# Keys of pair 5 transposed at the end of pair 4, between two stretches of feed-forward units

## Chip, cores and metric

The kernel runs on one core of one Trainium2 chip. The metric is the device time of one execution in microseconds (us), as a median over runs.

## What is computed

Attention over 4 batches of 8 heads, 768 positions and 64 values each, then a feed-forward block over the 3072 tokens that result:

```
scores = q @ k.T / sqrt(64)
mask   = causal                                  for heads 0, 2, 6   ("retrieval" heads)
         causal and (key < 4 or distance < 64)   for the other five  ("streaming" heads)
attn   = softmax(scores, masked) @ v             (4 x 8 x 768 x 64)
x      = attn, heads side by side                (3072 x 512)
h      = x @ w_in                                (3072 x 2048)
g      = max(h, 0) + alpha * min(h, 0)           (alpha: one number per column)
out    = g @ w_out                               (3072 x 512)
```

Inputs and output are float32; the kernel multiplies in bf16.

## The kernel before

Attention goes by pairs of heads: 16 pairs, n = 0 to 15, four in each batch, in the order (0,1), (2,3), (6,7), (4,5). Pair 4 is heads 0 and 1 of the second batch, pair 5 is heads 2 and 3. Each has a retrieval head first and a streaming head second. The work of a pair, by function:

- `load(n)` issues the loads of queries, keys and values (tiles `qf`, `kf`, `vf`) on SP's DMA queue. Up to pair 7, keys of each head are a DMA of their own.
- `whole_q(n)`, `whole_k(n)`, `whole_v(n)` cast them to bf16 (`natq`, `natm`, `vb`). POOL does it for pairs 1 to 5. For pairs 6 and 7 ScalarE (ACT) casts the queries (L162), VectorE (DVE) the keys (L175) and values (L189).
- `Tq(n)` and `Tk(n)`, for pairs up to 7, transpose queries and keys on TensorE (PE): six 128x128 transposes each (L265) into a PSUM bank. ScalarE copies the queries to `qT` (L275). Of the keys, ScalarE copies those of the first head to `kT` (L288) and, after it, VectorE those of the second (L292 to L294). From pair 8 on, DMAs transpose instead.
- `Sr(n,h,i)` and `Ss(n,h,i)`, short here for calls of `S_retr` and `S_stream`, compute one piece of the scores: matmuls with `kT` and `qT` (L333, L360) into one of two PSUM banks that alternate, an exponential on ScalarE (L341, L367), and a mask product on VectorE (L345, L371). From pair 4 on a retrieval head has six pieces, a streaming head three.
- `AV(n,h)` multiplies with the values (L387), then a reciprocal and a product on VectorE (L392, L393). `X(n)` transposes the pair's result (L400) into `xT` (L402).

The feed-forward part goes by token tiles t = 0 to 7, of 512 and 256 tokens in turn, in units. `P1(t,f)` is a block of the first matrix (L431), with a relu on ScalarE (L438) and one or two operations on VectorE (L441). `P2(t,s,u)` is a quarter of a 128-token row block of the second (L451); after the last quarter ScalarE copies the block (L456) and it is stored.

Every engine works through its instructions in the order in which the program issues them. For pairs 4 to 15 a planner sets that order. It has a list of *pieces* (the calls above, from `seg_pieces(n)`), with casts and loads ahead of pieces 0, 2 and 4 of a pair, and a list of *units*. It goes through the pieces. After each it adds to a budget the units left divided by the pieces left up to the next change of plan, and issues units while the budget holds half a unit's cost (L624 to L639). So a piece more, even an empty one, shifts all units up to the end of that plan a little. The first plan has 26 units and reaches into pair 8.

For pair 4 the order of pieces is written out by itself, since no pair before it overlaps:

```
sa + sb[:1] + [AV(4,0)] + [Tq(5), Tk(5)] + sb[1:]
```

with `sa` the six pieces of head 0 and `sb` the three of head 1. With the units that the planner puts between them, the program has from there on

```
AV(4,0)  P2(0,0,1)  Tq(5)  Tk(5)  P1(1,2)  Ss(4,1,1)  Ss(4,1,2)  P2(0,1,1)
whole_q(6)  Sr(5,0,0)  AV(4,1)  P2(0,0,2)  whole_k(6)  Sr(5,0,1)  Sr(5,0,2)  P1(1,4) ...
```

Of the kernel before, what the change touches and what calls it, by code (L numbers as in the profile page):

```python
# [14 lines left out]
def kernel(  # L15
# [51 lines left out]
    def bank(tag):  # L67
        return P[:, BANK[tag], :]
# [36 lines left out]
    def heads(n):  # L105
        return PAIRS[n % 4]
# [151 lines left out]
    def misc_tag():  # L258
        n_misc[0] += 1
        return f"m{n_misc[0] % 2}"  # L260
# [11 lines left out]
    def Tq(n):  # L272
        tr = T_bank(natq.pop(n), "mm0" if n < 4 else misc_tag())
        T = row_tokens(n)
        nc.scalar.copy(qT[n % NK][:, 0:S].rearrange("d (p t) -> d p t", t=T), in_order(tr[:, 0:S], T))  # L275

    def Tk(n):
        tr = T_bank(natk.pop(n), "mm1" if n < 4 else misc_tag())
        for hh, h in enumerate(heads(n)):
            T = row_tokens(n, h)  # L280
            rows = slice(64 * hh, 64 * hh + 64)
            kt = kTs[n % NK][hh][rows, :]
            src = in_order(tr[rows, 0:S], T)
            copy = nc.scalar.copy if n >= 4 and hh == 0 else nc.vector.tensor_copy
            if RETR[h]:
                cuts = [0, -(-256 // T), S // T] if n == 0 else [0, S // T]
                for lo, hi in zip(cuts, cuts[1:]):
                    copy(kt[:, 0:S].rearrange("d (p t) -> d p t", t=T)[:, lo:hi, :], src[:, lo:hi, :])  # L288
                continue
            slots = kt.rearrange("d (j m t) -> d j m t", j=7, t=T)  # L290
            a, z = NSINK // T, 748 // T
            copy(slots[:, 0:6, a:128 // T, :], src[:, a:z, :].rearrange("d (j m) t -> d j m t", j=6))  # L292
            nc.vector.tensor_copy(slots[:, 6, a:24 // T, :], src[:, z:S // T, :])
            nc.vector.tensor_copy(slots[:, :, 0:a, :], src[:, 0:a, :].unsqueeze(1).to_broadcast([64, 7, a, T]))  # L294
# [80 lines left out]
    def AV(n, hh):  # L375
        e, vv = ebuf.pop((n, hh)), vb[n % NV]
        pav = bank(misc_tag())[:, 0:NT * (D + 1)].rearrange("p (i c) -> p i c", c=D + 1)
        for i in range(NT):
            if RETR[heads(n)[hh]]:
                terms = [(RO[j] + QS[i] - QS[j], j) for j in range(min(i, 5) + 1)]  # L380
            elif i == 0:
                terms = [(0, 0)]
            else:
                own = SLOT * i + 4 if i < 6 else 5 * SLOT + 152
                terms = [(SLOT * (i - 1) + 128, i - 1), (own, i)]
            for m, (o, j) in enumerate(terms):
                nc.tensor.matmul(pav[:, i, :], e[:, o:o + 128], vv[:, j, hh, 0:D + 1],  # L387
                                 start=(m == 0), stop=(m == len(terms) - 1))
        if hh == 0:
            xn[n] = work.tile([128, NT, 128], bf16, tag="xn", name="xn")  # L390
        rcp = work.tile([128, NT, 1], fp32, tag=f"rcp{hh}", name="rcp")
        nc.vector.reciprocal(rcp, pav[:, :, D:D + 1])  # L392
        nc.vector.tensor_tensor(xn[n][:, :, 64 * hh:64 * hh + 64], pav[:, :, 0:D],  # L393
                                rcp.to_broadcast([128, NT, D]), op=ALU.mult)

    def X(n):
        nat = xn.pop(n)
        tr = bank_bf(misc_tag())
        for i in range(NT):
            nc.tensor.transpose(tr[:, QS[i]:QS[i] + 128], nat[:, i, :], ident)  # L400
        o = n // 4 % 2 * S
        nc.vector.tensor_copy(xT[:, n % 4, o:o + S], tr[:, 0:S])  # L402
# [79 lines left out]
    def seg_scores(n):  # L482
        parts = []
        for hh, h in enumerate(heads(n)):
            fn, m = (S_retr, N_R) if RETR[h] else (S_stream, 3)
            if n < 4:
                m = -(-m // 2)
            parts.append([lambda m=m, hh=hh, fn=fn: fn(n, hh, m) for m in range(m)])
        return parts

    def seg_pieces(n):
        sa, sb = seg_scores(n)

        prev = [lambda: AV(n - 1, 1)] if n > 4 else []
        tail = [lambda: X(n - 1)] if n > 4 else []
        nxt = [lambda: Tq(n + 1), lambda: Tk(n + 1)] if n + 1 < CROSS else []
        seq = sa[:1] + prev + sa[1:3] + tail + sa[3:5] + nxt[:1] + sa[5:] + nxt[1:] + sb[:1]
        seq += [lambda: AV(n, 0)] + sb[1:]
        if n == 4:
            seq = sa + sb[:1] + [lambda: AV(n, 0)] + nxt + sb[1:]  # L500
        return seq, (2 + len(sa[1:3]) if tail else 0)

    whole_q(0)
# [42 lines left out]
    for n in range(4):  # L546
        sa, sb = seg_scores(n)
        last = [lambda: AV(n - 1, 0), lambda: AV(n - 1, 1), lambda: X(n - 1)] if n else [None] * 3
        nxt = [lambda: Tq(n + 1), lambda: Tk(n + 1)] if n < 3 else [None] * 2
        if len(sa) == 3:  # L550
            seq = [sa[0], last[0], nxt[0], sa[1], last[1], nxt[1], sa[2], sb[0], last[2], sb[1]]
        else:
            seq = [sa[0], last[0], sa[1], last[1]] + sb + [lambda: AV(3, 0), last[2]]
        if n == 0:
            seq = sa[:2] + nxt[:1] + sa[2:] + nxt[1:] + sb
        if n == 0:
            seq += [slopes, factors]
        seq = [x for x in seq if x]
# [32 lines left out]
    for n in range(4, NSEG):  # L591
        seq, x_at = seg_pieces(n)
        for i, piece in enumerate(seq):
            pre = []
            if i in (0, 2, 4):
                fn = (whole_q, whole_k, whole_v)[i // 2]
                pre = [lambda m=m, fn=fn: fn(m) for m, lo, hi in ((n + 1, 5, CROSS), (n + 2, CROSS, NSEG)) if lo <= m < hi]
            if i == 4 and n < NSEG - NF:
                pre.append(lambda n=n: load(n + NF))
            ready = []  # L600
            if x_at and i == x_at - 1 and n % 4 == 0:
                ready = [n // 2 - 2, n // 2 - 1]
            pieces.append((pre, piece, ready))
# [75 lines left out]
```

## Time and profile before

| | us |
|---|---|
| median of 5 runs | 246.24 |
| the five | 245.63 to 246.52 |
| the profiled execution | 247.28 |
| its span, first to last instruction | 245.3 |
| PE busy in it | 232.7 (95%) |
| DVE, ACT, POOL busy | 165.5, 142.9, 48.7 |

The profile comes from one execution, which took 1.04 us more than the median of the others. Times in it count from the start of its span. A busy share of PE counts matmuls that overlap as one stretch. In the lists of groups and in the timeline a row gives the engine, the line of the kernel, the operation, what it writes and reads, and how many; in brackets stands the idle time of the engine before it and what released it. "PEld" is TensorE's weight load and "PEclk" the share of its clock that was granted. The page also cuts the span into 40 slices of 6.13 us, one digit each, in tenths.

### The profile page before, as it was taken

How to read it: one execution, taken by the hardware profiler on the slowest of the kernel's cores; microseconds unless marked ns; L12 is line 12 of the kernel's file. 1: busy time of each engine (PE TensorE's matmuls, PEld its weight loads, DVE VectorE, ACT ScalarE, POOL GpSimd, SP SyncE). 2: the span in 40 equal slices, each digit the busy share in tenths (PEclk: the TensorE clock that was granted, in tenths of full speed). 3: DMA queues.
4: the chain of work that ended last, by engine and by line, in shares of the span. 5: the costliest groups of instructions: out<-in, count | busy, mean ns of one | idle time of the engine just before them, and what ended most of it. 6: DMA issues, size and time to landing. Idle time of an engine off the chain costs nothing.

```text
span 245.3 us, 5348 instructions
## 1 busy us (share of the span) xinstructions
PE 232.7 (95%) x2059; PEld 146.6 (60%) x2059; DVE 165.5 (67%) x398; ACT 142.9 (58%) x255; POOL 48.7 (20%) x98
## 2 busy tenths in 40 slices
PE   7799899949999999999999999999999999999994
PEld 6688545636677645556766555556676544465553
DVE  7788788836789968888577767876665556542310
ACT  5888188656876658665554467765655255533320
POOL 5669610720230310201111100300000000000000
PEclk9999999988999999999999999999999999999999
DMA  7999999999999999999969930501111101012112
GB/s 223 283 238 171 226 201 204 243 262 250 244 217 140 246 155 229 222 181 230 182 143 175 229 83 9 141 3 43 45 43 47 43 0 43 3 43 85 46 44 86
DMA packets 85377, 34.95 MB, mean 142 GB/s; under 512 B 72536, under 2 KB 83560, under 8 KB 85352
## 3 DMA queue, kind: packets, MB, share of 16 engines
q1 hardware_dynamic: 79368, 25.36, 51.9%
q0 software_dynamic: 5664, 8.91, 16.3%
q10 hardware_dynamic: 320, 0.34, 0.5%
q8 instruction: 16, 0.26, 0.4%
q14 instruction: 9, 0.07, 0.1%
HBM read 27.46 MB, written 6.29 MB: 138 GB/s over the span
## 4 chain that ended last, share of the span: by engine, by line
PE 67%; DMA 12%; DVE 8%; SPq 5%; ACT 3%; issue 2%; POOL 2%; DVEq 0%; ACTq 0%; POOLq 0%
PE P L451 27%; PE P L431 26%; DMA kf<-in_k_dram 7%; PE P L387 5%; PE P L333 3%; DMA qf<-in_q_dram 3%; PE P L360 3%; DMA vf<-in_v_dram 2%; SPq L141 2%; SPq L139 2%; DVE g L441 2%; PE P L468 1%; DVE vb L189 1%; SPq L126 1%; ACT eR L341 1%
## 5 line engine op out<-in xcount | busy, mean ns | idle before, releaser
L441 DVE SCALAR_TENSOR_TENSOR g<-neg,oma,P 128x512 bf16<-128x512 f32 (+1 forms) x128 | 74.9, 612 | 49.7 <-ACT neg L438 48.2
L431 PE MATMUL P<-xT,w_in_b 128*128 128x512 bf16 (+1 forms) x512 | 96.2, 326 | 1.2 <-DVE xT L402 1.2
L451 PE MATMUL P<-w_out_b,g 128*128 128x512 bf16 x368 | 93.5, 382 | 0.0
L438 ACT ACTIVATE neg<-P 128x512 f32<-128x512 f32 x96 | 57.1, 597 | 54.3 <-PE P L431 50.7
L431 PEld LDWEIGHTS <-w_in_b 128*128 128x128 bf16 x512 | 48.2, 98 | 28.9
L451 PEld LDWEIGHTS <-g 128*128 128x128 bf16 x368 | 33.8, 98 | 29.0 <-issue 1.2
L341 ACT ACTIVATE eR<-P 128x455 bf16<-128x455 f32 (+3 forms) x63 | 37.4, 604 | 13.8 <-PE P L333 11.9
L367 ACT ACTIVATE eS<-P 128x384 bf16<-128x384 f32 (+1 forms) x55 | 27.7, 520 | 10.5 <-PE P L360 9.9
L459 POOL DMA_DIRECT2D out_dram<-ot x18 | 10.3, 574 | 100.8 <-ACT ot L456 93.5
L333 PE MATMUL P<-qT,kT 128*128 128x454 bf16 (+10 forms) x132 | 24.4, 271 | 1.1 <-DVE kT L288 0.5
L371 DVE TENSOR_TENSOR eS<-eS,ms 128x384 bf16<-128x384 bf16 (+1 forms) x47 | 17.8, 389 | 4.4 <-ACT eS L367 4.1
L360 PE MATMUL P<-qT,kT 128*128 128x192 bf16 (+2 forms) x140 | 20.0, 237 | 0.8 <-ACT eR L341 0.6
L393 DVE TENSOR_TENSOR xn<-P,rcp 128x448 bf16<-128x448 f32 x32 | 20.0, 625 | 1.1
L456 ACT COPY ot<-P 128x512 f32<-128x512 f32 x23 | 13.5, 585 | 10.4 <-PE P L451 10.4
L333 PEld LDWEIGHTS <-kT 128*128 128x128 bf16 x132 | 11.6, 98 | 11.6 <-issue 2.4
L360 PEld LDWEIGHTS <-kT 128*128 128x128 bf16 x140 | 13.2, 99 | 8.3 <-issue 0.3
L345 DVE TENSOR_TENSOR eR<-eR,mr 128x128 bf16<-128x128 bf16 (+4 forms) x54 | 11.6, 235 | 4.7 <-ACT eR L341 4.6
L387 PEld LDWEIGHTS <-eS 128*128 128x128 bf16 x260 | 11.0, 99 | 4.1 <-issue 0.8
L387 PE MATMUL P<-vb,eS 128*128 128x65 bf16 x260 | 12.3, 196 | 0.6 <-DVE eS L371 0.4
L387 PEld LDWEIGHTS <-eR 128*128 128x128 bf16 x324 | 11.3, 97 | 1.3
L387 PE MATMUL P<-vb,eR 128*128 128x65 bf16 x324 | 11.9, 192 | 0.0
L292 DVE COPY kT<-P 64x744 bf16<-64x744 bf16 x9 | 8.4, 933 | 4.2 <-ACT kT L288 4.0
(81 smaller groups left out, 157.8 us busy)
## 6 DMA issues: line engine op xcount, KB each, us to landing
qf<-in_q_dram SPq DMA_DIRECT2D x16, 384.0 KB
vf<-in_v_dram SPq DMA_DIRECT2D x32, 192.0 KB
kf<-in_k_dram SPq DMA_DIRECT2D x31, 192.0 KB
out_dram<-ot POOLq DMA_DIRECT2D x18, 256.0 KB, 3.1
w_in_b<-in_moe_w_in_dram POOLq DMA_DIRECT2D x4, 512.0 KB, 8.6
w_out_b<-in_moe_w_out_dram POOLq DMA_DIRECT2D x4, 512.0 KB, 19.4
out_dram<-ot SPq DMA_DIRECT2D x5, 256.0 KB
vf<-in_v_dram SPq DMA_DIRECT2D x20, 6.0 KB
```

The source lines that it names most:

```text
L333: nc.tensor.matmul(sc[:, x, a - lo:z - lo], kt[:, 128 * j:128 * (j + 1)], qt[:, c:c + z - a], start=True, stop=not masked)
L341: nc.scalar.activation(e[:, lo:hi].rearrange("p (x c) -> p x c", x=len(parts)), sc[:, 0:len(parts), 0:(hi - lo) // len(parts)], AF.Exp, sc ...
L360: nc.tensor.matmul(sc[:, x, o:o + w], kt[:, 128 * j:128 * (j + 1)], qt[:, 124 * j:124 * j + w], start=True, stop=not on_pe)
L367: nc.scalar.activation(slots, sc[:, 0:len(thirds), 0:384].rearrange("p x (s c) -> p x s c", c=192), AF.Exp, scale=scale)
L371: nc.vector.tensor_tensor(slots, slots, factor, op=ALU.mult)
L387: nc.tensor.matmul(pav[:, i, :], e[:, o:o + 128], vv[:, j, hh, 0:D + 1], start=(m == 0), stop=(m == len(terms) - 1))
L393: nc.vector.tensor_tensor(xn[n][:, :, 64 * hh:64 * hh + 64], pav[:, :, 0:D], rcp.to_broadcast([128, NT, D]), op=ALU.mult)
L431: nc.tensor.matmul(psg[:, w * i:w * (i + 1)], w_in_b[:, a, 128 * fb:128 * (fb + 1)], xT[:, c, o:o + w], start=(c == 0), stop=(c == 3))
L438: nc.scalar.activation(neg, psg, AF.Relu, scale=-1.0)
L441: nc.vector.scalar_tensor_tensor(g_buf[t % 2][:, fb, 0:w], neg[:, c], oma[:, fb:fb + 1], psg[:, c], op0=ALU.mult, op1=ALU.add)
L451: nc.tensor.matmul(bank(po[t, s]), g_buf[t % 2][:, f, 128 * s:128 * (s + 1)], w_out_b[:, f, :], start=(f == 0), stop=(f == 15))
L456: nc.scalar.copy(ot, bank(po.pop((t, s))))
```

## The change

The order of pieces for pair 4. `Tq(5)` stays behind `AV(4,0)`. `Tk(5)` goes behind the two remaining pieces of pair 4's second head, with an empty piece ahead of it and one behind it. Empty pieces issue nothing, but the planner may put units after them.

```diff
         if n == 4:
-            seq = sa + sb[:1] + [lambda: AV(n, 0)] + nxt + sb[1:]
+
+            seq = sa + sb[:1] + [lambda: AV(n, 0)] + nxt[:1] + sb[1:] + [lambda: None] + nxt[1:] + [lambda: None]
         return seq, (2 + len(sa[1:3]) if tail else 0)
```

By the planner's arithmetic the order of the program becomes

```
AV(4,0)  P2(0,0,1)  Tq(5)  Ss(4,1,1)  P1(1,2)  Ss(4,1,2)  P2(0,1,1)  Tk(5)  P2(0,0,2)
whole_q(6)  Sr(5,0,0)  AV(4,1)  P1(1,4)  whole_k(6)  Sr(5,0,1)  P2(0,1,2)  Sr(5,0,2)
whole_v(6)  load(9)  X(4)  Sr(5,0,3)  Sr(5,0,4)  P2(0,0,3)  Tq(6)  Sr(5,0,5)  P1(1,6)  Tk(6)  Ss(5,1,0) ...
```

and further units change places with the piece beside them up to `Tk(7)`. Which unit uses which PSUM bank stays as it was.

## The prediction

> **What bounds the kernel now.** I read the page first, then TensorE's waits, then the time around the change on TensorE, POOL and ScalarE, then stretches of one clock window each. The page's busy shares and slices:
>
> ```profile
> PE 232.7 (95%) x2059; PEld 146.6 (60%) x2059; DVE 165.5 (67%) x398; ACT 142.9 (58%) x255; POOL 48.7 (20%) x98
> ...
> PE   7799899949999999999999999999999999999994
> ...
> PEclk9999999988999999999999999999999999999999
> ```
>
> TensorE (PE) is busy almost everywhere, so the sum of its work and its gaps is the time. One slice after the start-up shows 4 tenths (the ninth, 49.1 to 55.2 us), and the only clock digits of 8 stand there and in the next slice. The waits of PE name the cause:
>
> ```profile
> PE P L265 <- POOL natm L175: 3.2, 1, 3.2
> ...
> PE P L387 <- DVE eS L371: 0.4, 1, 0.4
> ```
>
> One wait of 3.2 us: the transposes of `Tk(5)` for the cast of pair 5's keys. All other waits of PE after start-up are at most 0.6 us each. PE in order of time (start, length, idle before):
>
> ```profile
> 48.48 0.50 PE L265 MATMUL P<-ident,natq 128*128 128x128 bf16 x6
> 52.14 0.51 PE L265 MATMUL P<-ident,natm 128*128 128x128 bf16 x6 [3.16 <-POOL natm L175]
> 52.49 1.04 PE L431 MATMUL P<-xT,w_in_b 128*128 128x256 bf16 x8
> 53.36 0.74 PE L360 MATMUL P<-qT,kT 128*128 128x192 bf16 x5
> 53.92 1.88 PE L451 MATMUL P<-w_out_b,g 128*128 128x512 bf16 x4
> 55.60 0.59 PE L333 MATMUL P<-qT,kT 128*128 128x454 bf16 x1
> ```
>
> `Tq(5)` is followed by nothing until the keys come. Directly behind `Tk(5)` in PE's queue stands work that doesn't read them: `P1(1,2)` (L431), the last two score pieces of pair 4 (L360), `P2(0,1,1)` (L451). The keys' side, on POOL and on ScalarE:
>
> ```profile
> 51.58 0.51 POOL L175 CAST natm<-kf 128x384 bf16<-128x384 f32 x1 [2.77 <-DMA kf<-in_k_dram]
> ...
> 52.69 0.79 ACT L288 COPY kT<-P 64x768 bf16<-64x768 bf16 x1 [2.87 <-PE P L265]
> ...
> 54.85 0.84 ACT L162 CAST natq<-qf 128x768 bf16<-128x768 f32 x1
> ```
>
> The second head's keys land at 51.53 and POOL casts them at once. That time belongs to the DMA and not to PE, so PE being earlier or later doesn't move it. Stretches of 3.41 us (length; busy us of PE, PEld, DVE, ACT, POOL; clock; DMA share, GB/s) show the price behind the gap:
>
> ```profile
> 46.65:50.06 3.41, 2.32 (x39) 1.52 (x36) 3.06 (x7) 1.46 (x3) 2.16 (x4) 1.00 1.20 231
> 50.06:53.47 3.41, 1.33 (x16) 1.24 (x17) 0.00 (x0) 0.78 (x1) 0.51 (x1) 1.00 1.08 309
> 53.47:56.88 3.41, 3.41 (x25) 2.03 (x23) 2.62 (x8) 2.63 (x6) 1.27 (x2) 0.50 0.74 193
> ```
>
> After the stretch with PE busy for 1.33 of 3.41 us (39%) the clock is halved for a whole stretch, while PE has work throughout: 3.41 x 0.5 = 1.7 us lost. After the stretch with 2.32 us (68%) it is not. That is why the L451 group above takes 1.88 us instead of the usual 1.02.
>
> **What the Trainium skill says.** "TensorE: Matmul & The Clock Gate", Part 1, says that the clock is set by a free-running window of 3413 ns and falls to one half after an idle window. The trace agrees on length and half rate; it differs on "idle", since 39% of busy time was not enough here, and the measurement decides. The same page's specification table calls ScalarE and VectorE strict FIFOs, on which I rely where a cast that waits for a transfer holds up an exponential behind it. The trace lists both engines' instructions in program order at this place, which agrees but doesn't prove it.
>
> **The change part by part.** It removes and adds no instruction: the two empty pieces emit nothing. The planner's spacing of units shifts, which I worked out by following its arithmetic: bank names stay the same, and the order differs only from `Tk(5)` to about `Tk(7)`.
>
> 1. *The gap.* By start times the gap is from 48.48 + 0.34 = 48.82 to 52.14, 3.32 us. Now `Ss(4,1,1)`, `P1(1,2)`, `Ss(4,1,2)`, `P2(0,1,1)` stand in it. At full clock, from rows of the same shapes elsewhere: 0.17 + 0.87 + 0.17 + 0.86 = 2.07 us, to 50.89. Their inputs are ready: the values of g(0) long since, score banks free at 47.3. `Tk(5)` still starts at 52.14, so 1.25 us of gap stays. **Gain 2.07 us.**
>
> 2. *The clock.* The stretch from 50.06 to 53.47 then holds 1.33 + 0.83 = 2.2 us of PE, 63%, close to the 68% that kept the clock, and far from 39%. I take it that the clock stays full: **gain 1.70 us**. The bounds are 0 (63% doesn't do) and 1.7.
>
> 3. *Keys to scores.* Before, three pieces and units covered the copies of kT. Now only `P2(0,0,2)` does (52.49 to 53.35). ScalarE's copy for the first head ends at 52.69 + 0.79 = 53.48, so `Sr(5,0,0)` starts at about 53.54: **loss 0.19 us**. The second head's copies on DVE (end 54.65 before) are needed only at 60 us. With the cover gone altogether the cost would be 1.05 us.
>
> 4. *The queries of pair 6.* The cast `whole_q(6)` on ScalarE stands ahead of `Sr(5,0,0)`'s exponential. The landing record of the trace (the increments of each transfer's semaphore) has these queries at 54.51; before, ScalarE came there at 54.85 and didn't wait, now it comes at 53.48. So the cast runs from 54.55 to 55.39, the exponential (0.55) to about 55.85. On PE: `Sr(5,0,0)` to 53.74, `AV(4,1)` 0.39 to 54.13, `P1(1,4)` 0.87 to 55.00, `Sr(5,0,1)` to 55.19. `Sr(5,0,2)` needs the first one's score bank (two alternate), so it starts at 55.90: **loss 0.71 us**. Bounds: nothing if the queries land 0.7 us sooner, 1.2 if 0.5 later.
>
> 5. *Behind that.* `Sr(5,0,2)` to 56.10, `P2(0,1,2)` to 56.96, `X(4)` to 57.35 (its input is ready at 56.86: exponential, mask 0.22, reciprocal 0.20, product 0.62 on DVE), two scores to 57.75, `P2(0,0,3)` to 58.61, `Tq(6)` to 58.95, one score to 59.15, `P1(1,6)` to 60.02, `Tk(6)` to 60.36. Then comes `Ss(5,1,0)`, with the same work done as before, where it starts at 63.17: 2.81 us earlier, which agrees with the parts so far (2.87). In DVE's queue the cast of pair 6's keys comes at about 57.6, as before; they land at 55.64.
>
> 6. *A longer chain at `X(5)`.* The planner now puts `P1(1,8)` ahead of `AV(5,1)`, where it stood behind it. PE reaches the end of `P1(1,8)` at 60.36 + 0.17 + 0.86 + 0.81 (`AV(5,0)`) + 0.17 + 0.86 + 0.17 + 0.19 + 0.87 = 64.46. ScalarE meanwhile does the exponential of `Ss(5,1,2)` (to 64.05), the cast of pair 7's queries (0.84, to 64.8), the exponential of `Sr(6,0,0)` (to 65.3) and the relu of `P1(1,8)` (0.60, to 65.85); each starts some 0.05 us before the one ahead has ended, as in the rows of before. DVE then does the two operations of `P1(1,8)` (0.87 together, to 66.75) ahead of reciprocal and product of `AV(5,1)` (to 67.55). PE would come to `X(5)` at 66.1 (`AV(5,1)` 0.39, two scores 0.39, `P2(0,3,0)` 0.86), or 66.3 with a short wait of `AV(5,1)` for its mask, and waits until 67.6. Before, `X(5)` started at 69.65 without a wait. **The lead shrinks from 2.81 to 2.05 us, a loss of 0.76**; before lost 0.74 us in gaps on this way (the 0.4 us wait for a mask in it), now 1.5. Bounds: nothing lost if the relu is served sooner, 1.2 if ScalarE is further behind. The other swaps of neighbours have nothing behind them that waits, and PE's queue is full there: nothing. `Tk(7)` had 0.26 us of idle before it, which I leave as it is.
>
> 7. *Loads and queues.* SP's issues are paced by earlier landings at this place, and no load is moved. POOL's queue keeps its order. PE's lead is then checked against landings: values of pair 8 land at 68.29, their cast would move from about 71.8 to 69.7; keys of pair 10 at 82.78 against 86.43 - 2.1 = 84.3; values of pair 10 at 84.29 against 87.10 - 2.1 = 85.0. All stay ahead; a lead of over 2.8 would be cut at the last one, with `X(7)` behind it on DVE and `P1(2,0)` behind that. From there on PE is fed to the end, and the lead stays.
>
> Sum: 2.07 + 1.70 - 0.19 - 0.71 - 0.76 = 2.11 us. The profiled execution took 247.28 us (span 245.3), 1.04 above the median 246.24. Its own sum gives 245.2; from the median, 246.24 - 2.1 = **244.1 us**.
>
> **The rivals.**
>
> *A. The clock still falls* for a stretch (63% isn't enough), or in the ordinary runs it doesn't fall before either. For it: the threshold is bracketed only by 39 and 68%, and the profiled run is 1.04 us above the median. Against it: 63% is near the upper one, and the five runs lie within 0.9 us, less than one halved stretch. With the new stretch at half rate PE does `Sr(5,0,0)`, `AV(4,1)`, `P1(1,4)` in twice the time, which hides the wait for pair 6's queries, so the loss against the forecast is 1.0 and not 1.7: gain 1.1, 245.1 us. If the ordinary runs of before had a full clock, it is 2.11 - 1.70 = 0.4 us, 245.8.
>
> *B. The new waits don't come*: neither queries of pair 6 nor `X(5)` is late. 2.07 + 1.70 - 0.19 = 3.6, cut at pair 10's values to about 3.2: 243.0. Against it: 54.51 in the record, and the order in item 6.
>
> *C. The lead is given back*: transfers turn out to be what all waits for (slices show DMA 9 tenths busy up to 115 us). No change, 246.2. Against it: no wait of DVE or ScalarE for a load anywhere in the trace before.
>
> *D. Slower*: ScalarE is held at the queries of pair 6. The loss of item 4 is landing + 1.39 - 55.19; with item 6 it exceeds the 3.6 us of items 1 to 3 from a landing at 56.6 on. At 58 it is 4.2 + 0.8 = 5.0 against 3.6: 247.6. Against it: 54.51, and an issue at 47.08.
>
> That `Tk(5)` isn't moved at all is excluded by the code.
>
> **How the numbers follow.** The forecast (gain 1.4 to 2.8) has 0.66, A 0.15, B 0.10, C 0.04, D 0.05. A measurement of this kernel can tell about 0.2%, 0.5 us, from no change; a fifth of A lies under that. Faster: 0.66 + 0.12 + 0.10 = 0.88; same 0.07; slower 0.05. The range goes from 243.0 (B) to 245.6, past A's likelier half.
>
> **What would show it.** Right: PE's wait for POOL natm falls to about 1.1 to 1.3 us; no clock digit of 8 in the ninth and tenth slices; ScalarE shows a wait for qf ahead of L162 of about 1 us and PE one of about 0.7 at L333; `Ss(5,1,0)` near 60.4; a wait of about 1.2 us of PE at L400 for L393 near 67. Wrong: a half-clock stretch after 53 us (A), no wait for qf and none at L400 (B), waits of DVE for loads after 65 us (C), or a wait for qf of over 2 us (D). A cast of pair 5's keys that moves itself by over 0.5 us would upset items 1 to 4 together.

## The result and the profile after

The kernel after takes 244.67 us (median of 44 executions, 244.01 to 245.58), the kernel before 245.91 (79 executions, among them the five shown ahead). The ratio is 0.9943, 95% interval 0.9931 to 0.9954: a gain of 1.4 us by this ratio and of 1.24 by the medians, where 2.1 were forecast. The profiled execution went from 247.28 to 245.15, its span from 245.3 to 242.9.

The two rows of the page that showed the loss, PE's busy slices and its clock:

```profile
PE   7799899899999999999999999999999999999994
...
PEclk9999999999999999999999999999999999999999
```

The 4 in the ninth slice is an 8 now, and no slice has a clock digit of 8. The waits of PE, of the same view as ahead (who waited for whom, total, times, longest):

```profile
PE P L400 <- DVE xn L393: 1.4, 2, 0.9
...
PE P L387 <- DVE eR L345: 1.0, 1, 1.0
```

The wait for `POOL natm` is not in the list any more. Two waits are new: one of 0.93 us ahead of `X(5)`, forecast, which lengthens the row of L400 (0.8 us in two waits before, the longest 0.5), and one inside `AV(4,0)` at L387, not forecast. PE in order of time (start, length, idle before):

```profile
48.89 0.39 PE L387 MATMUL P<-vb,eR 128*128 128x65 bf16 x7 [1.01 <-DVE eR L345]
49.11 1.02 PE L451 MATMUL P<-w_out_b,g 128*128 128x512 bf16 x4
49.98 0.50 PE L265 MATMUL P<-ident,natq 128*128 128x128 bf16 x6
50.31 0.33 PE L360 MATMUL P<-qT,kT 128*128 128x192 bf16 x2
50.48 1.04 PE L431 MATMUL P<-xT,w_in_b 128*128 128x256 bf16 x8
51.35 0.33 PE L360 MATMUL P<-qT,kT 128*128 128x192 bf16 x3
51.52 1.02 PE L451 MATMUL P<-w_out_b,g 128*128 128x512 bf16 x4
52.38 0.50 PE L265 MATMUL P<-ident,natm 128*128 128x128 bf16 x6
52.72 1.03 PE L451 MATMUL P<-w_out_b,g 128*128 128x512 bf16 x4
53.77 0.37 PE L333 MATMUL P<-qT,kT 128*128 128x454 bf16 x1
...
60.25 0.33 PE L360 MATMUL P<-qT,kT 128*128 128x192 bf16 x2
...
67.37 0.56 PE L400 MATMUL P<-ident,xn 128*128 128x128 bf16 x7 [0.93 <-DVE xn L393]
```

The four groups from 50.31 to 52.38 are the two score pieces, `P1(1,2)` and `P2(0,1,1)`: 2.07 us of work between `Tq(5)` and `Tk(5)`, as forecast. `Tk(5)` no longer waits. POOL cast the keys 1.19 us earlier in this execution than in the profile before (51.58), and had done by 50.90:

```profile
50.39 0.51 POOL L175 CAST natm<-kf 128x384 bf16<-128x384 f32 x1 [1.65 <-DMA kf<-in_k_dram]
```

`Ss(5,1,0)` starts at 60.25, where 60.36 was forecast, `X(5)` at 67.37, where 67.6 was. ScalarE's wait for pair 6's queries is there as well:

```profile
54.35 0.83 ACT L162 CAST natq<-qf 128x768 bf16<-128x768 f32 x1 [0.64 <-DMA qf<-in_q_dram]
```

So the order of events came out close to the forecast, and the gain of the profiled execution too (2.13 against 2.11 us). In part this is luck. `Tq(5)` starts 1.50 us later than in the profile before (49.98 against 48.48), mostly for the wait in `AV(4,0)`; and as the keys came sooner, the 1.25 us that PE was still to wait ahead of `Tk(5)` are gone. The two nearly cancel: `Tk(5)` starts at 52.38, where 52.14 was forecast. The gain of the medians is smaller, and the experiments were made to see why.

### The profile page after: what moved, and what is told of

It reads as the page before. It is cut to its first block, busy times and chain, and to the rows that moved or that the text cites. A ratio compares the mean times of both kernels' runs of the same rounds, so it can differ in the third digit from the quotient of the medians.

```text
span 242.9 us, 5348 instructions
## 1 busy us (share of the span) xinstructions
PE 231.8 (95%) x2059; PEld 146.1 (60%) x2059; DVE 165.1 (68%) x398; ACT 142.5 (59%) x255; POOL 48.6 (20%) x98
## 4 chain that ended last, share of the span: by engine, by line
PE 64%; SPq 12%; DVE 10%; DMA 6%; ACT 4%; issue 2%; POOL 0%; DVEq 0%; ACTq 0%; POOLq 0%
PE P L451 26%; PE P L431 25%; SPq L139 7%; DMA qf<-in_q_dram 5%; PE P L387 4%; PE P L333 4%; SPq L141 3%; PE P L360 2%; DVE g L441 2%; ACT eR L341 1%; PE P L468 1%; DVE vb L189 1%; DMA vf<-in_v_dram 1%; DVE xT L402 1%; DVE kT L292 1%
## 5 line engine op out<-in xcount | busy, mean ns | idle before, releaser
L333 PE MATMUL P<-qT,kT 128*128 128x454 bf16 (+10 forms) x132 | 24.2, 269 | 1.2 <-DVE kT L288 0.5
L371 DVE TENSOR_TENSOR eS<-eS,ms 128x384 bf16<-128x384 bf16 (+1 forms) x47 | 16.6, 361 | 6.0 <-ACT eS L367 5.6
L333 PEld LDWEIGHTS <-kT 128*128 128x128 bf16 x132 | 11.3, 97 | 11.3 <-issue 2.4
L345 DVE TENSOR_TENSOR eR<-eR,mr 128x128 bf16<-128x128 bf16 (+4 forms) x54 | 12.4, 249 | 4.9 <-ACT eR L341 4.9
L387 PE MATMUL P<-vb,eR 128*128 128x65 bf16 x324 | 12.1, 193 | 1.0 <-DVE eR L345 1.0
L387 PEld LDWEIGHTS <-eR 128*128 128x128 bf16 x324 | 11.4, 97 | 2.7 <-DVE eR L345 1.1
L387 PEld LDWEIGHTS <-eS 128*128 128x128 bf16 x260 | 10.6, 97 | 3.6 <-DVE eS L371 0.6
L387 PE MATMUL P<-vb,eS 128*128 128x65 bf16 x260 | 12.0, 193 | 0.7 <-DVE eS L371 0.5
L400 PE MATMUL P<-ident,xn 128*128 128x128 bf16 x112 | 8.9, 219 | 1.4 <-DVE xn L393 1.4
```

What stands on the lines that cost most here:

```text
L333: nc.tensor.matmul(sc[:, x, a - lo:z - lo], kt[:, 128 * j:128 * (j + 1)], qt[:, c:c + z - a], start=True, stop=not masked)
L371: nc.vector.tensor_tensor(slots, slots, factor, op=ALU.mult)
```

## The experiments

The ratios are to executions of the kernel before that ran beside each set; intervals are 95%.

### How often the clock falls: the kernel before twice more, and a filler

The runs list the mean clock of each execution. Of the kernel before there are 153 beside the experiments. Forty-nine have 0.990 to 0.993, the mark of one half-clock stretch (1.7 us lost in 245 are 0.7%), with a median of 247.20 us. A hundred have 0.997 or more, median 245.88 (four at 0.985 or less, with 248.9 to 250.1 us, are left out). For the 79 executions of the result no clock is on record. Of the 44 of the kernel after none is under 0.998. Among its variants below, two of 22 (one empty piece and a second cast) and one of 11 (memsets moved) have 0.991 to 0.993; which gap does it there, no profile shows. Two more profiles of the kernel before:

> The kernel before once more, for a profile of another of its executions. Theory: about two in three of them have a full clock; in such a one the wait for pair 5's keys is shorter or is split by a wait ahead of it, and the time is 245 to 246.5. Rival: the wait is 3.2 us in every execution.

> The same, for one more execution: a full clock with 245 to 246.5 us, or a half-clock stretch after a wait of 3 us and 247 us.

The first took 247.19 us, the second 246.84. PE of the first, then of the second:

```profile
49.23 0.51 PE L265 MATMUL P<-ident,natq 128*128 128x128 bf16 x6 [0.48 <-POOL natq L162]
52.04 0.51 PE L265 MATMUL P<-ident,natm 128*128 128x128 bf16 x6 [2.30 <-POOL natm L175]
```

```profile
49.29 0.51 PE L265 MATMUL P<-ident,natq 128*128 128x128 bf16 x6 [0.77 <-POOL natq L162]
51.97 0.51 PE L265 MATMUL P<-ident,natm 128*128 128x128 bf16 x6 [2.17 <-POOL natm L175]
...
55.69 0.59 PE L387 MATMUL P<-vb,eS 128*128 128x65 bf16 x9 [0.74 <-DVE eS L371]
```

The wait is 2.2 to 2.3 us there, not 3.2, because `Tq(5)` already waited for POOL's cast of the queries. The clock of the first is halved from 53.12 to 56.53, that of the second isn't. The second is a slow one of its kind: only eight of the hundred with a full clock took as long, so the usual wait of these isn't shown. In each trace the stretches can be counted from the first entry of the clock record: in the profile ahead it stands at 5.68 us, and the fall at 53.47 is 14 stretches of 3.41 us (3413 ns) later. The stretch that holds the wait, in the first and in the second (columns as ahead):

```profile
49.71:53.12 3.41, 1.11 (x14) 1.01 (x14) 0.00 (x0) 1.33 (x2) 0.51 (x1) 1.00 1.05 283
```

```profile
49.98:53.40 3.42, 1.43 (x17) 1.34 (x18) 0.06 (x1) 1.45 (x2) 0.59 (x2) 1.00 1.11 306
```

PE was busy for 1.11 us (33%) in the one, 1.43 (42%) in the other. The point lies between the 39% of the first profile and 42%. The ends of the profiles agree: a last stretch with PE busy for 25 to 32%, in five of them, is followed by half a clock, one with 56 or 57%, in two, isn't. Nearly the same gap falls on either side of the point, by where the stretches happen to lie. The second profile shows one thing more: with a full clock `AV(4,1)` waits 0.74 us for the last mask of pair 4.

The filler gives PE something useless to do in the wait:

```diff
     def Tk(n):
+        if n == 5:
+            fill = bank(f"sc{(n_sc[0] + 1) % 2}")
+            for _ in range(10):
+                nc.tensor.matmul(fill, ident, xT[:, 0, 0:512], start=True, stop=True)
         tr = T_bank(natk.pop(n), "mm1" if n < 4 else misc_tag())
```

> The kernel before, with ten matmuls of 512 columns (about 2.1 us), whose results nobody reads, put between Tq(5) and Tk(5), where the kernel after has P1(1,2), P2(0,1,1) and the scores. They keep PE busy in the wait and do none of its work: it shows the share of the clock by itself. Theory (the half-clock stretch follows from the gap): no execution has a mean clock of 0.993 or less, and the time is that of the executions of the kernel before with a full clock, 245.5 to 246.2, or up to 0.5 us more where the keys come early. Rival (the clock has another cause): about a third of the executions keep a clock of 0.993 or less, and the times still reach 247 to 248.

246.35 us, ratio 0.9999 (0.9979 to 1.0019); none of 22 executions under 0.997. The matmuls take the place of the wait:

```profile
49.41 2.32 PE L281 MATMUL P<-xT,ident 128*128 128x512 bf16 x10
51.70 0.51 PE L265 MATMUL P<-ident,natm 128*128 128x128 bf16 x6
```

The clock follows from the lack of work there, then: none of 22 has the mark, where a third of the executions of before have it. The median is still no better. It is 0.4 us above that of the full-clock executions of before in its own set (245.96), and no run shows why: in this profile the keys were ready only at 51.64, so the filler cost nothing ahead of `Tk(5)`. Keeping the clock up is not what makes the kernel after faster in most executions: there it is the new order. The profile shows a wait in `AV(4,1)` as well (L391 is L387 of the other kernels):

```profile
55.50 0.59 PE L391 MATMUL P<-vb,eS 128*128 128x65 bf16 x9 [0.82 <-DVE eS L375]
```

### The place of Tk(5), or the spacing of the units

```diff
-            seq = sa + sb[:1] + [lambda: AV(n, 0)] + nxt + sb[1:]
+            seq = sa + sb[:1] + [lambda: AV(n, 0)] + nxt + sb[1:] + 2 * [lambda: None]
```

> Tk(5) stays at its old place behind Tq(5); only the two empty pieces are added, at the end of pair 4. From pair 5 on the order of the program is that of the kernel after. Theory (the gain is work put into the wait for pair 5's keys): PE still waits for the cast of the keys by 2 to 3.3 us, and pays the later X(5) of the new spacing besides, so the time is that of the kernel before or up to 0.8 us more, 245.8 to 246.7. Rival (the gain comes from the planner's new spacing of units): as the kernel after, about 244.6.

245.54 us, ratio 0.9989 (0.9959 to 1.002), with two of 14 executions at half clock. From pair 5 on this order is that of the kernel after, and it can't be told from the kernel before (0.3 us under the range given; the rival's 244.6 is 0.9 off). Its profile has a short wait, the keys having landed early and `AV(4,0)` late:

```profile
50.51 0.51 PE L265 MATMUL P<-ident,natm 128*128 128x128 bf16 x6 [0.41 <-POOL natm L175]
```

So one profile of it would have misled: its span (243.1) is within 0.2 us of the one after, its median isn't. `Tk(5)` alone, with no empty piece:

```diff
+            seq = sa + sb[:1] + [lambda: AV(n, 0)] + nxt[:1] + sb[1:] + nxt[1:]
```

> Tk(5) behind the last two score pieces of pair 4 with no empty piece. One unit (P1(1,2)) and the scores stand in the wait, 1.2 us of work in place of 2.07; P2(0,1,1) follows as cover of the key copies; behind it the spacing of the kernel before, with AV(5,1) ahead of P1(1,8). Theory: 0.86 us less cover than in the kernel after, but no later X(5) (0.76 us in the prediction's sum, PE's wait at L400 0.9 us in the profile after): 244.4 to 245.1, about as the kernel after. Rival (both empties are needed for the gain): about as the kernel before, over 245.4.

245.19 us, ratio 0.9963 (0.9945 to 0.9982), 0.1 us above what the theory gave. The move alone brings about two thirds of the gain (0.37% of 0.57%, with intervals that overlap). PE still waits 0.84 us for the keys in its profile, and one of 22 executions has the half clock. The rest would be the empty pieces': they put a second unit into the wait, `P2(0,1,1)`, and another behind `Tk(5)`.

### Nothing to wait for

Both kernels with the cast keys of pair 4 transposed in place of pair 5's:

```diff
-        tr = T_bank(natk.pop(n), "mm1" if n < 4 else misc_tag())
+        tr = T_bank(NATK1[0] if n == 5 else natk.pop(n), "mm1" if n < 4 else misc_tag())
```

> The order of the kernel before, but Tk(5) transposes the cast keys of pair 4, which have been there long since, so that nothing waits for pair 5's keys (the scores of pair 5 then use the wrong keys; all sizes are the same). It shows what the wait was worth. Theory: the clock stays full and the gap goes, but ScalarE now stands at pair 6's queries (they land near 54.3 us) and PE at Sr(5,0,2) until about 55.9, against 57.9 in the profile before: a gain of 1 to 2 us, 244 to 245. Rival (the wait was the only bound there): 3.3 us and the half-clock stretch both gone, 241.5 to 243.

> The kernel after, with Tk(5) transposing pair 4's cast keys, so that nothing is left to wait for there (the scores of pair 5 use the wrong keys). Theory: the rest of the wait for keys, 0 to 1.2 us, only moves to the wait for pair 6's queries, so the time is that of the kernel after within 0.3 us, 244.3 to 244.9. Rival (what was left of the wait for keys still costs): 1 us less, 243.6.

In the order of before: 245.49 us, ratio 0.9964 (0.994 to 0.9988), 0.5 us above the range that the theory gave and over 2 us above the rival's. Four of its 22 executions still have the half clock, though nothing waits for pair 5's keys; which gap does it there, no profile shows. So the wait for these keys need not be behind every half-clock stretch of the kernel before. In the order of after: 244.41, ratio 0.9928 (0.9899 to 0.9957), not to be told from the kernel after. With no wait for keys in either, the order still makes 1.1 us of difference between the medians, 0.8 if the half-clock executions of the first are left out (the intervals of the ratios overlap a little). The profile of the first shows a reason:

```profile
53.24 0.28 PE L387 MATMUL P<-vb,eS 128*128 128x65 bf16 x4
54.51 0.59 PE L387 MATMUL P<-vb,eS 128*128 128x65 bf16 x9 [0.98 <-DVE eS L371]
```

`AV(4,1)` waits 0.98 us for a mask. VectorE of this profile, then of the profile after:

```profile
52.16 0.94 DVE L292 COPY kT<-P 64x744 bf16<-64x744 bf16 x1 [1.85 <-ACT kT L288]
...
53.31 0.87 DVE L441 SCALAR_TENSOR_TENSOR g<-neg,oma,P 128x256 bf16<-128x256 f32 x2
54.10 0.62 DVE L371 TENSOR_TENSOR eS<-eS,ms 128x384 bf16<-128x384 bf16 x2
```

```profile
53.02 0.35 DVE L371 TENSOR_TENSOR eS<-eS,ms 128x384 bf16<-128x384 bf16 x1
53.74 0.94 DVE L292 COPY kT<-P 64x744 bf16<-64x744 bf16 x1 [0.38 <-ACT kT L288]
```

In the old order VectorE has the key copies of `Tk(5)` (L292 to L294, from 52.16 to 53.29) and the products of `P1(1,2)` ahead of the last masks of pair 4, and the masks are done at 54.7. In the new order the masks stand ahead of the key copies; the profile after has no wait in `AV(4,1)`, and neither has the second of this pair. This is a part of the gain that I hadn't seen: the profile before had shown no such wait, because its PE ran at half clock there and came later.

### The two losses forecast

The cast of pair 6's queries was to be moved three pieces later in pair 5. The edit missed a line: piece 0 kept its cast, and a second one was added.

```diff
-            if i in (0, 2, 4):
+            if n == 5 and i in (2, 3, 4):
+                pre = [lambda fn=(whole_k, whole_q, whole_v)[i - 2]: fn(6)]
+            elif i in (0, 2, 4):
```

> The kernel after, with the cast of pair 6's queries on ScalarE three pieces later, behind the exponentials of Sr(5,0,0) and Sr(5,0,1). In the profile after ScalarE waits 0.64 us there for the transfer and PE some 0.4 us at Sr(5,0,2). Theory (item 4 of the prediction: that wait costs): 0.2 to 0.5 us less than the kernel after, 244.2 to 244.5. Rival (the later wait at X(5) swallows it): as the kernel after, 244.7.

245.19 us, ratio 0.9949 (0.9926 to 0.9973), above both figures given. But this doesn't test the theory; it says that 0.83 us more of ScalarE's time in this place costs nothing that the ratios can tell from the kernel after. The cast really moved, and nowhere else:

```diff
-            if i in (0, 2, 4):
+            if n == 5 and i < 5:
+                pre = [lambda fn=fn: fn(6) for fn in (None, None, whole_k, whole_q, whole_v)[i:i + 1] if fn]
+            elif i in (0, 2, 4):
```

> The kernel after, with the cast of pair 6's queries really moved: it stands behind the exponentials of Sr(5,0,0) and Sr(5,0,1) on ScalarE and nowhere else (in the run meant for this the first cast had stayed in its place and a second one was added). Theory (item 4 of the prediction: the wait for these queries costs PE 0.3 to 0.7 us): 0.2 to 0.6 us less than the kernel after, a ratio of about 0.992 to the kernel before, 244.1 to 244.5. Rival (ScalarE's later work is as late as before, so that the wait only moves): as the kernel after, a ratio of 0.994, 244.7. A cast that comes too late for Tq(6) would show as a wait of PE at L265 and a higher time.

244.71 us, ratio 0.9932 (0.9913 to 0.9951): the median is the rival's, the ratio lies between the two, and neither can be told from the kernel after. In the profile, which is of a late execution (245.47 us, with 1.51 us of wait at `Tq(5)`), ScalarE does not wait for the queries any more, and `Sr(5,0,2)` follows at once on PE. But two scores later PE waits for a bank all the same:

```profile
56.07 1.02 PE L451 MATMUL P<-w_out_b,g 128*128 128x512 bf16 x4
56.93 0.55 PE L400 MATMUL P<-ident,xn 128*128 128x128 bf16 x7
57.32 0.36 PE L333 MATMUL P<-qT,kT 128*128 128x45 bf16 x2
58.20 0.35 PE L333 MATMUL P<-qT,kT 128*128 128x106 bf16 x2 [0.52 <-ACT eR L341]
```

The cast now stands ahead of the exponential that frees this bank. In this profile the wait has moved with the cast, as the rival has it.

One empty piece less gives `AV(5,1)` its place ahead of `P1(1,8)` back. It was run so, and with the second cast of the first of these edits:

```diff
-            ... + nxt[:1] + sb[1:] + [lambda: None] + nxt[1:] + [lambda: None]
+            ... + nxt[:1] + sb[1:] + [lambda: None] + nxt[1:]
```

> The kernel after with one empty piece in place of two, ahead of Tk(5). Tk(5) keeps its cover, P1(1,2) and P2(0,1,1); P2(0,0,2) goes behind Sr(5,0,0), and at pair 6 AV(5,1) stands ahead of P1(1,8) again. Theory (item 6 of the prediction: the order of these two costs 0.76 us at X(5)): PE's wait at L400, 0.93 us in the profile after, is gone; against it the copies of the keys lie open for up to 0.9 us ahead of Sr(5,0,0), which the wait for pair 6's queries would have cost anyway in part: 243.9 to 244.5. Rival (the open copies cost as much as X(5)): 244.7 or more.

> Both: one empty piece, and the cast of pair 6's queries three pieces later. Theory: neither the wait for the queries nor X(5) is left: 243.7 to 244.3, the best of these. Rival (the open copies of the keys decide here): no better than with one of them.

245.6 us, ratio 0.9967 (0.9951 to 0.9983), and 245.51, ratio 0.9962 (0.9939 to 0.9984). Both miss by over 1 us (the second, having the cast twice, tells no more than the first); the interval of the first touches that of the kernel after only at its end. The profile of the first:

```profile
53.42 0.36 PE L333 MATMUL P<-qT,kT 128*128 128x454 bf16 x1 [0.88 <-ACT kT L288]
...
65.29 0.59 PE L387 MATMUL P<-vb,eS 128*128 128x65 bf16 x9 [0.83 <-DVE eS L371]
```

Without `P2(0,0,2)` behind `Tk(5)`, PE waits 0.88 us for ScalarE's copy of the keys. And with `AV(5,1)` ahead of `P1(1,8)` it is `AV(5,1)` that waits, 0.83 us, in place of `X(5)`. The second empty piece gives the copies their cover.

### POOL's casts and the wait in AV(4,0)

In the profile after, three small mask products on VectorE take 1.75 us (start, length); on POOL two casts run at the same time:

```profile
47.09 1.75 DVE L345 TENSOR_TENSOR eR<-eR,mr 128x136 bf16<-128x136 bf16 x3
```

```profile
47.48 0.81 POOL L162 CAST natq<-qf 128x768 bf16<-128x768 f32 x1
48.25 0.50 POOL L175 CAST natm<-kf 128x384 bf16<-128x384 f32 x1
```

In the second of the new profiles of before the casts come a microsecond later (48.42), and the same three products take 0.51 us. The last product ends at 48.84, 0.09 us after the second cast. In the profile ahead, where POOL's casts ran from 47.55 to 48.82, it was the next product that took long (0.34 us elsewhere), and PE did not stand for it:

```profile
47.34 1.68 DVE L371 TENSOR_TENSOR eS<-eS,ms 128x384 bf16<-128x384 bf16 x1
```

The Trainium skill, "SBUF — State Buffer", section "Who interferes with whom", says that a VectorE operation with two SBUF inputs and a GpSimd operation that reads SBUF exclude each other for the whole instruction; this agrees. POOL's six memsets were therefore put ahead of the cast of pair 4's values, where POOL waits for a transfer anyhow:

```diff
     whole_k(4)
-    whole_v(4)
     for i in range(NF):
         nc.gpsimd.memset(kf[i][:, 6, :, :], 0.0)
     for nat in NATK:
         nc.gpsimd.memset(nat.bitcast(fp32), 0.0)
+    whole_v(4)
```

> The kernel after, with POOL's six memsets (2.4 us) put ahead of the cast of pair 4's values, into the 9.8 us in which POOL waits for these. POOL then comes to the casts of pair 5's queries and keys up to 2.4 us sooner, as far as they have landed. Theory (these casts, coming when they do, hold up VectorE's mask products: three of them take 1.75 us in the profile after, and PE waits 1.0 us for them in AV(4,0)): the wait at L387 goes or moves, 0 to 1 us less, 243.8 to 244.7. Rival (the landings decide): as the kernel after.

244.98 us, ratio 0.9941 (0.9911 to 0.997): 0.3 us above the theory's range, and not to be told from the kernel after, as the rival has it. The wait is still there, 0.63 us in place of 1.01, since the casts now start as the queries land, 47.01 against 47.48. Over all fourteen profiles the two waits take turns. Where POOL starts the cast of pair 5's queries at 46.5 to 47.6 us, `AV(4,0)` waits 0.63 to 1.12 us in six of seven; where it starts at 48.15 or later, `AV(4,0)` does not wait, and `Tq(5)` waits 0.48 to 1.51 us for the cast in six of seven. No version that computes the same result could be told to be faster than the kernel after.

## Why the prediction was right, and where its sizes were off

Faster was right, and the range holds the result, in part by luck. About two thirds of the executions of before have no clock to win back (item 2), and for these the prediction's own sum is a gain of 0.4 us, 245.8, outside its range. That the result lies inside goes with smaller losses in items 4 and 6 and with a wait that the sum does not have (item 7). Of the signs that were to show a right forecast, no half-clock stretch is left, but the wait for the keys is 0 in place of 1.1 to 1.3 us, and the others came smaller (0.64 for about 1 on ScalarE, some 0.25 for about 0.7 at L333, 0.93 for about 1.2 at L400). The sign that would upset items 1 to 4 together, pair 5's keys moving by over 0.5 us, came too. By its own items:

1. *The gap.* Right in kind: `Tk(5)` no longer holds PE, 2.07 us of work stand ahead of it, and with `Tk(5)` in its old place (the empties alone) no gain can be told. The 3.32 us were one execution's: the other profiles of before have waits of 2.17 and 2.30 us. POOL's cast of the second head's keys started anywhere from 49.4 to 52.3 us over the profiles of these kernels, so it was wrong to take that time for fixed, whether or not PE moves it.
2. *The clock.* The mechanism was right, the size was the term mis-sized. It was counted at 1.70 us in every execution; it occurs in 49 of 153, and costs 247.20 - 245.88 = 1.32 us there. That is 0.42 us on the mean of these, and 0.46 on their median (246.34 for all). The 79 executions of the result have a median of 245.91, near that of a full clock. Rival A had this variant, "if the ordinary runs of before had a full clock", and gave it 0.4 us of gain. Between full-clock executions the gain is 245.88 - 244.67 = 1.2 us, so that was too low in turn; 4, 6 and the mask in 7 show where more can come from.
3. *Keys to scores.* As forecast: by start times `P2(0,0,2)` is over at 52.72 + 0.86 = 53.58, and `Sr(5,0,0)` starts at 53.77, 0.19 us later. With the cover taken away it was 0.88, where 1.05 was forecast.
4. *Queries of pair 6.* The wait came (0.64 us on ScalarE), its price of 0.71 us did not: PE stood for about 0.25 us at `Sr(5,0,2)` in the profile after (0.80 for a group that takes 0.55 elsewhere), and moving the cast away moved the wait two scores on. The step that failed is to take the delay of one score for a delay of the whole. That ScalarE has the same work to do in any order would explain it; the runs do not settle it.
5. *The path to `Ss(5,1,0)`* was right to 0.11 us, with the later `Tq(5)` and the earlier keys cancelling ahead of it.
6. *`X(5)`.* From `Ss(5,1,0)` to `X(5)` the new order takes 7.12 us, the old 6.48 in the profile before and 6.47 in two experiments: 0.64 lost, 0.76 forecast. From there to `Ss(6,1,0)` it takes 4.27 against 4.51, so 0.24 comes back, which I had left at nothing. The experiment that undid it had a nearly equal wait at `AV(5,1)`.
7. *Loads and queues.* VectorE waits for no load in the profile after, and the lead stays: 73.29 - 70.78 = 2.51 us at `P2(0,3,1)`, 2.4 in the span. What the item left out is VectorE's queue at `Tk(5)`. With the key copies ahead of the masks of pair 4, `AV(4,1)` waits in three full-clock profiles (0.74 us in the second of before, 0.82 with the filler, 0.98 with pair 4's keys), and with the empties alone its matmuls take 1.01 us in place of 0.55; with the copies behind them it does not. That the order is worth about 1 us without any wait for keys is shown by the last pair; that the mask makes up this 1 us is a reading of its profiles, since no run moves the copies alone. How much of the 1.2 us is this and how much the gap, no run tells.

Of rival A, the first form did not occur (no half clock in 44 executions), and the second is the case in two thirds of the executions beside the experiments. Rivals B, C and D did not occur: the wait for the queries was there, the lead stayed, and no wait for the queries exceeded 1.03 us in any profile.

## What to carry to other kernels

Where an engine waits for a transfer, look for work that stands behind the waiting instruction and does not need it, and move as much as the wait is long; leave one unit behind the moved step as cover for its copies. When a step is moved, look at every engine's queue: here the step's copies on VectorE, moved behind the masks, seem to have counted as well as its matmuls. And ask how often a profiled state occurs: the clock loss of 1.7 us in one profile was there in a third of the executions.

## What was not expected of the hardware

The clock fell for 3.41 us after a stretch of 3.41 us with TensorE busy for 39% (1.33 us) or 33% (1.11), and did not after one with 42% (1.43): in these traces no wholly idle stretch was needed, and gaps of 2.2 and 2.3 us can fall on either side. Three mask products that take 0.51 us together took 1.75 when they met casts on POOL.
